# Attention and maxout on one core: group 3's q is loaded ahead of w1's second half, V follows its cast, and two pads and a relu change engines

## The chip, the cores and the metric

The kernel runs on one core of a Trainium2 chip. The metric is device time in microseconds of one execution. Engines are named as in the profile: PE is TensorE, DVE is VectorE, ACT is ScalarE, POOL is GpSimd, SP is SyncE. SP does no arithmetic here, it only issues transfers.

## The reference

Attention over 8 batches, 8 heads, 576 positions and head size 64, with a causal mask by blocks of 64, followed by a maxout layer over the 4608 tokens:

```python
scores = (1.0 / np.sqrt(D)) * np.matmul(q, k.transpose(0, 1, 3, 2))
scores = np.where(block_i >= block_j, scores, -1000000000.0)
attn = exp(scores - max) / (sum + 1e-09)
x = np.matmul(attn, v)              # then (B * S, H * D) = (4608, 512)
g = np.maximum(x @ w1, x @ w2)      # d_ff = 1024
out = g @ w_out                     # (4608, 512), float32
```

The kernel writes max(h1, h2) as relu(x (w1 - w2)) + x w2, so that the last step is `relu(x d) w_out + x m` with `d = w1 - w2` and `m = w2 w_out`, both made on the chip.

## The kernel before

**The work.** Heads are taken in pairs p = 0 to 31, four to a batch, and two pairs make a group g = 0 to 15. A group's q and k come from memory as float32 in one 576 KB transfer each (`load_qk`, L107), are cast to bf16 (`cast`, L147), transposed on PE (`transposes`, L358, 18 small matmuls for q and 18 for k) and copied out of PSUM (L372). Scores go through `tile_0`, `tile_1` and `tile_2` (L446 to L472) into PSUM and through exp on ACT (L407) into `aT`; POOL clears the masked corners (`mask`, L411). `av` (L482) multiplies by V and divides by the sum. `tile_2` reads `kz`, a copy of two key blocks with zeros between them, which `pad_keys` (L389) makes for each pair. V is loaded a batch at a time in five parts (`load_v`, L157), from POOL's queue.

**The maxout layer.** `load_w1` (L175) loads w1 in two halves of 1 MB from SP's queue. `diff_w(j)` (L184, j = 0 to 3) subtracts a quarter of w2 from a quarter of w1 on DVE. `h_unit(i, f)` (L226, f = 0 to 7) makes 128 of the 1024 columns of the relu for 512 tokens, in four matmuls (L233) and a relu out of PSUM (L238); f = 0 and 1 need `diff_w(0)`, 2 and 3 `diff_w(1)`, and so on. `m_unit` and `bT_unit` make `m`; `y_unit` makes 128 rows of the result. PSUM tiles of all these steps, the transposes' too, are taken in turn from one pool of four buffers (`ps_m`, tag "m"), so that a step waits until the tile four before it has been read out.

**The order.** Each engine runs its instructions in the order in which this program writes them (`manual_schedule`, L86). `fill(n)` (L334) takes the next units of the maxout layer from a list, whatever is ready, for about n matmuls of 512 columns; so attention's steps are written out by hand and the holes between them are filled. From L591 to L691 the first four groups are written out; from L693 a loop takes groups 3 to 15.

**What gates a transfer.** With `gated`, `load_qk` first writes one element of the new buffer with a memset, on POOL or on the engine given, and SP's transfer waits for it. A transfer is thereby placed behind what stands ahead of the memset on that engine:

```python
            if gated:
                (nc.gpsimd if gated is True else gated).memset(t[:, 0, :1], 0.0)
```

SP issues its transfers in program order, and a transfer that waits holds those behind it.

**Around the change.** Before, SP issues q and k of group 2, both halves of w1, then q and k of group 3, one behind the other. POOL casts q of group 2, issues two of V's parts for batch 1, pads pairs 4 and 5, issues the other three parts, clears the gates of group 4, and casts q and k of group 3. DVE runs `diff_w(0)`, `diff_w(1)`, a relu, `diff_w(2)`, a relu, `diff_w(3)`, two relus.

Of the kernel before, what the change touches and what calls it, by code (L numbers as in the profile page):

```python
# [10 lines left out]
AF = mybir.ActivationFunctionType  # L11
# [3 lines left out]
def kernel(  # L15
# [10 lines left out]
    nc = tc.nc  # L26
# [17 lines left out]
    RPP = S // NP  # L44
# [9 lines left out]
    NCH = 5  # L54
# [50 lines left out]
    dve, pool, act = nc.vector.tensor_copy, nc.gpsimd.tensor_copy, nc.scalar.copy  # L105

    def load_qk(g, queues, gated=False):  # L107
        b, u = divmod(g, GPB)
        for nm, src, queue in (("q", q, queues[0]), ("k", k, queues[1])):
            if queue is None or by_dma(nm, g):  # L110
                continue
            raws[nm, g] = t = raw.tile([P, 2, RPP * D], FP32, name=f"{nm}raw")
            if gated:
                (nc.gpsimd if gated is True else gated).memset(t[:, 0, :1], 0.0)
            queue.dma_start(
                out=t[:],
                in_=src[b, 4 * u:4 * u + 4].rearrange(
                    "(s h) (p t) d -> (h p) s (t d)", h=2, t=RPP),
            )
# [4 lines left out]
    def by_dma(nm, g):  # L124
        return g >= T_DMA.get(nm, NG)
# [21 lines left out]
    def cast(nm, g, parts):  # L147
        if by_dma(nm, g):
            return
        t = raws[nm, g].rearrange("p s (t d) -> p t s d", d=D)  # L150
        if (nm, g) not in qk_n:
            qk_n[nm, g] = qkn.tile([P, RPP, 2, D], BF16, name=f"{nm}n")
        n = qk_n[nm, g]
        for copy, j0, j1 in parts:
            copy(out=n[:, j0:j1], in_=t[:, j0:j1])  # L155

    def load_v(b, c):  # L157
        rows = min(P, S - c * P)
        nc.gpsimd.dma_start(  # L159
            out=vv_r[b % NV][P - rows:, c, :, :D],  # L160
            in_=v[b, :, c * P:c * P + rows, :].rearrange("h p d -> p h d"),
        )
# [12 lines left out]
    def load_w1(i):  # L175
        t = wraw.tile([P, NDM, 2 * WB], FP32, name="w1raw")
        nc.sync.dma_start(out=t[:], in_=w1r[:, :, 2 * i * WB:2 * (i + 1) * WB])
        for j in range(2):
            w1_raw[2 * i + j] = t[:, :, j * WB:(j + 1) * WB]
# [4 lines left out]
    def diff_w(j):  # L184
        nc.vector.tensor_sub(d_sb[:, :, j * WB:(j + 1) * WB], w1_raw[j], w2_sb[j])  # L185
# [8 lines left out]
    dve, pool, act = nc.vector.tensor_copy, nc.gpsimd.tensor_copy, nc.scalar.copy  # L194
    SP, ACT = nc.sync, nc.scalar
# [30 lines left out]
    def h_unit(i, f):  # L226
        if f == 0:
            g_tiles[i] = g_pool.tile([P, NFF, SPAN], BF16, name="g")
        g = g_tiles[i]
        t0 = i * SPAN  # L230
        pt = ps_m.tile([P, SPAN], FP32, name="ps_h", tag="m")
        for c in range(NDM):
            nc.tensor.matmul(  # L233
                pt[:], d_sb[:, c, f * P:(f + 1) * P], xT[:, c, t0:t0 + SPAN],
                start=(c == 0), stop=(c == NDM - 1),
            )
            if c == NDM - 1:
                nc.vector.tensor_scalar_max(g[:, f], pt[:], 0.0)  # L238
            yield

    def bT_unit(j):
# [92 lines left out]
    def fill(n):  # L334
        while n > 0:
            if not current:
                k = next((k for k, t in enumerate(todo) if t[2] <= done_tokens[0]), None)
                if k is None:
                    return max(0, n)
                current.append(todo.pop(k))  # L340
            t = current[0]
            next(t[1])
            n -= t[3]
            t[0] -= 1
            if not t[0]:
                current.pop()
        return 0
# [10 lines left out]
    def transposes(nm, g, copies):  # L358
        n = qk_n.pop((nm, g))
        pts = [ps_m.tile([P, RPP, NP], BF16, name=f"ps_{nm}T", tag="m") for _ in range(2)]  # L360
        for j in range(RPP):
            for i in range(2):
                r = slice(i * NP, (i + 1) * NP)
                nc.tensor.transpose(  # L364
                    pts[i][:, j, :], n[r, j].rearrange("p s d -> p (s d)"), ident[r, r],
                )

        def copy_out(which=(0, 1), part=(0, NP), copy=None):
            p0, p1 = part
            for i in which:  # L370
                t = (qT_r if nm == "q" else kT_r)[(2 * g + i) % NT]
                (copy or copies[i])(  # L372
                    out=t[:, p0 * RPP:p1 * RPP].rearrange("q (p j) -> q p j", j=RPP),
                    in_=pts[i][:, :, p0:p1].rearrange("q j p -> q p j"),
                )
        return copy_out

    def scores(p, ps, col, c, q0, w):
        qT, kT = qT_r[p % NT], kT_r[p % NT]
        k0 = min(c * P, S - P)  # L380
        for hh in range(2):
            r = slice(hh * D, (hh + 1) * D)
            nc.tensor.matmul(  # L383
                ps[:, hh, col:col + w], kT[r, k0:k0 + P], qT[r, q0:q0 + w],
                start=True, stop=True,
            )


    def pad_keys(p):  # L389
        nc.gpsimd.tensor_copy(  # L390
            out=kz_r[p % NT].rearrange("p (a c) -> p a c", c=BLK)[:, 0:3:2],
            in_=kT_r[p % NT][:, S - 3 * BLK:].rearrange("p (a c) -> p a c", c=BLK)[:, 0:3:2],
        )


    def corner_scores(p, ps, col):
        qT, kz = qT_r[p % NT], kz_r[p % NT]
        for k0, q0 in ((0, 384), (BLK, 512)):
            for hh in range(2):
                r = slice(hh * D, (hh + 1) * D)  # L400
                nc.tensor.matmul(  # L401
                    ps[:, hh, col:col + BLK], kz[r, k0:k0 + P], qT[r, q0:q0 + BLK],
                    start=(k0 == 0), stop=(k0 > 0),
                )

    def exp(p, ps, w, a0):
        nc.scalar.activation(  # L407
            out=aT_r[p % NA][:, :, a0:a0 + w], in_=ps[:, :, :w], func=AF.Exp, scale=scale,
        )

    def mask(p, a0, eng=None):  # L411
        (eng or nc.gpsimd).memset(aT_r[p % NA][BLK:, :, a0:a0 + BLK], 0.0)  # L412
# [33 lines left out]
    def tile_0(p):  # L446
        u = ps_s.tile([P, 2, 512], FP32, name="ps_s", tag="s")
        scores(p, u, 0, 0, 0, 512)
        return lambda masked: (exp(p, u, 512, 0), masked and mask(p, 0))
# [7 lines left out]
    def tile_2(p):  # L457
        u = ps_s.tile([P, 2, 512], FP32, name="ps_s", tag="s")
        corner_scores(p, u, 320)
        scores(p, u, 0, 2, 256, 320)  # L460
        scores(p, u, 384, 3, 448, P)

        def out(masked):
            exp(p, u, 512, 1024)
            nc.scalar.activation(
                out=aT_r[p % NA][BLK:, :, 1536:AW], in_=u[BLK:, :, 320:320 + BLK],
                func=AF.Exp, scale=scale,
            )
            if masked:
                mask(p, 1024)  # L470
                mask(p, 1344)
        return out  # L472

    def masks(p):
        for a0 in (0, 576, 1024, 1344):
            mask(p, a0)

    def region(*tiles, masked=True):
        for out in tiles:
            out(masked)  # L480
# [157 lines left out]
    load_qk(2, (SP, None), gated=nc.vector)  # L638
    load_qk(2, (None, SP))
    load_w1(0)  # L640
    load_w1(1)
    load_qk(3, (SP, SP))
    av(2, [2, 3, 4])
    burst_q3(3)
    mask(3, 1408)
# [1 line left out]
    x_out(0)  # L647
    av(3, [0, 1])
    cast("q", 2, ((pool, 0, RPP),))
    load_v(1, 0)  # L650
    load_v(1, 1)
    fill(8)
    av(3, [2, 3, 4])
    fill(8)
    x_out(1, 0, NCH, (act, dve))
    fill(4)
    transposes("q", 2, (dve, act))()
    cast("k", 2, ((act, 0, RPP),))
    fill(8)
    diff_w(0)  # L660
    diff_w(1)
    transposes("k", 2, (act, act))()
    pad_keys(4)
    pad_keys(5)
    for c in range(2, NCH):
        load_v(1, c)
    fill(4)
    load_qk(4, (SP, SP), gated=True)
    cast("q", 3, ((pool, 0, RPP),))
    cast("k", 3, ((pool, 0, RPP),))  # L670
    region(tile_0(4), tile_1(4), masked=False)
    fill(4)
    diff_w(2)
    fill(4)
    region(tile_2(4), tile_0(5), masked=False)
    diff_w(3)
    masks(4)
    fill(8)
    copy_out = transposes("q", 3, (dve, act))
    outs = tile_1(5), tile_2(5)  # L680
    copy_out()
# [1 line left out]
    fill(4)  # L683
    transposes("k", 3, (dve, act))()
    pad_keys(6)
    pad_keys(7)
    masks(5)
# [90 lines left out]
```

## Time and profile before

| | |
|---|---|
| median of 4 runs | 255.62 us (255.4 to 257.37) |
| profiled execution | 255.83 us |
| its span | 254.0 us |
| PE busy | 239.7 us, 94% |
| DVE, ACT, POOL busy | 150.8, 119.9, 119.2 us |
| granted PE clock | 1.0 |

The span runs from the first instruction to the last; the rest of the execution's time lies around it. Busy times are of each engine by itself, so they add up to far more than the span. DMA busy is the mean over 16 DMA engines. Times in the timelines count from the start of the span.

### The profile page before, as it was taken

The page shows a single profiled execution, that of the slowest core. Times are in us where ns is not written, and L with a number is a line of the kernel's source. Part 1 is how long each engine was busy: PE and PEld are TensorE (multiplying, and loading weights), DVE is VectorE, ACT ScalarE, POOL GpSimd, SP SyncE. Part 2 cuts the span into 40 slices and gives each one's busy share as a digit, 9 for nine tenths or more (in the row PEclk, how much of TensorE's full clock was granted, in tenths as well). Part 3 has the DMA queues.
Part 4 walks back from the last instruction along what each step waited for, and adds up shares of the span by engine and source line. Part 5 has one row for each costly group of instructions (what it writes and reads, how often), then busy time and mean ns, then how long its engine had stood idle before and what let it go on. Part 6 is the DMA issues. An engine that isn't in the chain of part 4 may idle for free.

```text
span 254.0 us, 6697 instructions
## 1 busy us (share of the span) xinstructions
PE 239.7 (94%) x2728; PEld 132.7 (52%) x2763; DVE 150.8 (59%) x303; ACT 119.9 (47%) x158; POOL 119.2 (47%) x280
## 2 busy tenths in 40 slices
PE   8787998998999999999999999999999999999995
PEld 3356853655455554545454545454545564444444
DVE  4977689666485367636753675357535754754521
ACT  2893297757675564646464646464645400000001
POOL 1970467579759556854685477547231100000000
PEclk9999999999999999999999999999999999999999
DMA  7999999699899999999999999999961311102123
GB/s 247 240 158 236 395 284 215 201 107 220 160 132 214 154 233 168 205 158 225 148 225 159 226 138 216 159 224 146 119 128 62 93 38 69 62 8 77 41 91 116
DMA packets 104863, 41.27 MB, mean 162 GB/s; under 512 B 89216, under 2 KB 93696, under 8 KB 104832
## 3 DMA queue, kind: packets, MB, share of 16 engines
q0 software_dynamic: 65376, 9.77, 57.7%
q1 hardware_dynamic: 39040, 30.42, 51.2%
q10 hardware_dynamic: 416, 0.66, 0.7%
q8 instruction: 21, 0.34, 0.6%
q14 instruction: 10, 0.08, 0.1%
HBM read 34.60 MB, written 9.44 MB: 173 GB/s over the span
## 4 chain that ended last, share of the span: by engine, by line
PE 85%; DMA 5%; DVE 4%; POOL 2%; issue 2%; ACT 1%; ACTq 0%
PE ps_y L275 35%; PE ps_h L233 24%; PE ps_o L498 11%; PE ps_s L383 8%; PE ps_M L256 3%; DMA vv<-in_v_dram 3%; DMA qraw<-in_q_dram 2%; PE ps_qT L364 2%; POOL vv L159 1%; DVE d_sb L185 1%; PE ps_y L290 1%; ACT aT L407 1%; PE ps_s L401 1%; PE ps_kT L364 1%; POOL xT L182 1%
## 5 line engine op out<-in xcount | busy, mean ns | idle before, releaser
L407 ACT ACTIVATE aT<-ps_s 128x1024 bf16<-128x1024 f32 (+2 forms) x100 | 95.6, 994 | 43.7 <-PE ps_s L383 30.6
L275 PE MATMUL ps_y<-wo_sb,g 128*128 128x512 bf16 x262 | 66.9, 379 | 2.6 <-issue 2.5
L233 PE MATMUL ps_h<-xT,d_sb 128*128 128x512 bf16 x277 | 66.9, 379 | 1.8 <-DVE g L238 0.8
L238 DVE TENSOR_SCALAR g<-ps_h 128x512 bf16<-128x512 f32 x72 | 49.5, 689 | 16.8 <-PE ps_h L233 16.8
L412 POOL MEMSET aT<- 64x128 bf16 x128 | 22.5, 199 | 63.5 <-ACT aT L407 62.8
L280 DVE COPY y<-ps_y 128x512 f32<-128x512 f32 x35 | 24.2, 691 | 45.9 <-PE ps_y L275 45.1
L498 PEld LDWEIGHTS <-aT 128*128 128x128 bf16 x960 | 37.4, 98 | 14.1 <-issue 0.4
L233 PEld LDWEIGHTS <-d_sb 128*128 128x128 bf16 x288 | 26.5, 98 | 32.1 <-issue 3.8
L275 PEld LDWEIGHTS <-g 128*128 128x128 bf16 x280 | 24.8, 98 | 30.2 <-issue 5.4
L498 PE MATMUL ps_o<-vv,aT 128*128 128x65 bf16 x960 | 39.7, 194 | 0.0
L275 PE MATMUL ps_y<-m_sb,xT 128*128 128x512 bf16 x135 | 37.3, 379 | 0.4 <-issue 0.2
L159 POOL DMA_DIRECT2D vv<-in_v_dram x40 | 33.9, 857 | 0.5
L383 PE MATMUL ps_s<-qT,kT 64*128 64x128 bf16 (+6 forms) x344 | 31.2, 280 | 2.9 <-ACT aT L407 1.1
L505 DVE TENSOR_TENSOR xp<-ps_o,rec 128x256 bf16<-128x256 f32 (+1 forms) x64 | 31.4, 491 | 2.2
L132 POOL DMA_DIRECT2D kb<-in_k_dram x40 | 29.4, 759 | 0.0
L504 DVE RECIPROCAL rec<-ps_o 128x4 f32<-128x4 f32 (+1 forms) x64 | 11.9, 187 | 25.4 <-PE ps_o L498 24.9
L295 ACT COPY y<-ps_y 128x256 f32<-128x256 f32 (+1 forms) x2 | 0.6, 319 | 49.3 <-PE ps_y L290 49.3
L155 POOL CAST qn<-qraw 128x1152 bf16<-128x1152 f32 (+1 forms) x15 | 16.5, 1102 | 11.2 <-DMA qraw<-in_q_dram 10.3
L372 ACT COPY qT<-ps_qT 128x576 bf16<-128x576 bf16 x15 | 9.6, 638 | 24.2 <-PE ps_qT L364 22.8
L275 PEld LDWEIGHTS <-xT 128*128 128x128 bf16 x140 | 12.7, 98 | 13.8 <-issue 0.8
L383 PEld LDWEIGHTS <-kT 64*128 64x128 bf16 x344 | 12.0, 94 | 13.3 <-issue 8.3
L372 DVE COPY qT<-ps_qT 128x576 bf16<-128x576 bf16 x17 | 12.7, 748 | 0.3 <-PE ps_qT L364 0.2
(57 smaller groups left out, 131.7 us busy)
## 6 DMA issues: line engine op xcount, KB each, us to landing
qraw<-in_q_dram SPq DMA_DIRECT2D x16, 576.0 KB, 5.0
out_dram<-y SPq DMA_DIRECT2D x35, 256.0 KB, 3.5
vv<-in_v_dram POOLq DMA_DIRECT2D x32, 128.0 KB, 6.1
kraw<-in_k_dram SPq DMA_DIRECT2D x5, 576.0 KB, 7.7
kb<-in_k_dram POOLq DMA_DIRECT2D x40, 72.0 KB, 6.4
w1raw<-in_moe_w_dram SPq DMA_DIRECT2D x2, 1024.0 KB, 10.7
xT<-in_moe_w_dram POOLq DMA_DIRECT2D x4, 256.0 KB, 6.5
wo_sb<-in_moe_w_out_dram POOLq DMA_DIRECT2D x2, 512.0 KB, 12.5
```

The source lines that it names most:

```text
L132: nc.gpsimd.dma_start(out=n[h * BLK:(h + 1) * BLK, :, s], in_=(q if nm == "q" else k)[b, 4 * u + 2 * s + h].rearrange("(j p) d -> p j d", ...
L159: nc.gpsimd.dma_start(out=vv_r[b % NV][P - rows:, c, :, :D], in_=v[b, :, c * P:c * P + rows, :].rearrange("h p d -> p h d"),)
L233: nc.tensor.matmul(pt[:], d_sb[:, c, f * P:(f + 1) * P], xT[:, c, t0:t0 + SPAN], start=(c == 0), stop=(c == NDM - 1),)
L238: nc.vector.tensor_scalar_max(g[:, f], pt[:], 0.0)
L275: nc.tensor.matmul(py[:], lhs, rhs, start=(n == 0), stop=(n == len(terms) - 1),)
L280: nc.vector.tensor_copy(out=y[:], in_=py[:])
L372: (copy or copies[i])(out=t[:, p0 * RPP:p1 * RPP].rearrange("q (p j) -> q p j", j=RPP), in_=pts[i][:, :, p0:p1].rearrange("q j p -> q p j"),)
L383: nc.tensor.matmul(ps[:, hh, col:col + w], kT[r, k0:k0 + P], qT[r, q0:q0 + w], start=True, stop=True,)
L407: nc.scalar.activation(out=aT_r[p % NA][:, :, a0:a0 + w], in_=ps[:, :, :w], func=AF.Exp, scale=scale,)
L412: (eng or nc.gpsimd).memset(aT_r[p % NA][BLK:, :, a0:a0 + BLK], 0.0)
L498: nc.tensor.matmul(po[:, gi, hh, :], a[:, hh, a0:a0 + P], vv[:, c, h0 + 2 * hh, :], start=(mm == 0), stop=(mm == n_mm - 1),)
L505: nc.vector.tensor_mul(xp[:, :, ts[0]:ts[0] + n, p % 2].rearrange("q s t d -> q t s d"), po[:, :, :, :D], rec[:, :n].to_broadcast([P, n, 2 ...
```

## The change

It touches the hand-written stretch before the loop only. SP's row of loads is written in two parts: q, k of group 2 and w1's first half as before; then, later in the program, q of group 3 with a gate on POOL behind group 2's cast, w1's second half, and k of group 3. The cast of group 3's q follows on POOL, and behind it all five parts of V for batch 1. Pads 4 and 5 go to DVE. The relu of `h_unit(0, 3)` goes to ACT. Two calls change place: the cast of group 2's k on ACT is written ahead of the transposes of its q, and `diff_w(3)` is written 4 units later. The matmuls and their order on PE are the same.

```diff
@@ h_unit
             if c == NDM - 1:
-                nc.vector.tensor_scalar_max(g[:, f], pt[:], 0.0)
+                if i == 0 and f == 3:
+                    nc.scalar.activation(out=g[:, f], in_=pt[:], func=AF.Relu)
+                else:
+                    nc.vector.tensor_scalar_max(g[:, f], pt[:], 0.0)
...
-    def pad_keys(p):
-        nc.gpsimd.tensor_copy(
+    def pad_keys(p, copy=pool):
+        copy(
...
     load_qk(2, (SP, None), gated=nc.vector)
     load_qk(2, (None, SP))
     load_w1(0)
-    load_w1(1)
-    load_qk(3, (SP, SP))
     av(2, [2, 3, 4])
...
     x_out(0)
     av(3, [0, 1])
     cast("q", 2, ((pool, 0, RPP),))
-    load_v(1, 0)
-    load_v(1, 1)
+    load_qk(3, (SP, None), gated=True)
+    load_w1(1)
+    load_qk(3, (None, SP))
+    cast("q", 3, ((pool, 0, RPP),))
+    for c in range(NCH):
+        load_v(1, c)
     fill(8)
     av(3, [2, 3, 4])
     fill(8)
     x_out(1, 0, NCH, (act, dve))
     fill(4)
+    cast("k", 2, ((act, 0, RPP),))
     transposes("q", 2, (dve, act))()
-    cast("k", 2, ((act, 0, RPP),))
     fill(8)
     diff_w(0)
     diff_w(1)
     transposes("k", 2, (act, act))()
-    pad_keys(4)
-    pad_keys(5)
-    for c in range(2, NCH):
-        load_v(1, c)
+    pad_keys(4, dve)
+    pad_keys(5, dve)
     fill(4)
     load_qk(4, (SP, SP), gated=True)
-    cast("q", 3, ((pool, 0, RPP),))
     cast("k", 3, ((pool, 0, RPP),))
     region(tile_0(4), tile_1(4), masked=False)
     fill(4)
     diff_w(2)
     fill(4)
     region(tile_2(4), tile_0(5), masked=False)
+    masks(4)
+    fill(4)
     diff_w(3)
-    masks(4)
-    fill(8)
+    fill(4)
     copy_out = transposes("q", 3, (dve, act))
```

## The prediction

> **What bounds the kernel now.** I read the page first, then the busy time by stretches, the waits, the chain in order of time, and the timelines of single queues. In all of them a group g is a pair of head pairs (2g, 2g+1); q3 and k3 are the q and k of group 3, h0 to h7 the eight `h_unit` calls of token span 0.
>
> ```profile
> span 254.0 us, 6697 instructions
> PE 239.7 (94%) x2728; PEld 132.7 (52%) x2763; DVE 150.8 (59%) x303; ACT 119.9 (47%) x158; POOL 119.2 (47%) x280
> DMA  7999999699899999999999999999961311102123
> ```
>
> TensorE is busy 94% of the span, and its matmuls are the same in both programs and in the same order. The change can only fill or widen TensorE's holes. The stretches say how large those are where the change lies (columns: length, then busy time of PE, PEld, DVE, ACT, POOL, then granted clock, DMA share, GB/s):
>
> ```profile
> 23.00:34.00 11.00, 9.63 (x150) 7.80 (x150) 7.19 (x17) 3.67 (x6) 3.06 (x4) 1.00 1.08 372
> 34.00:46.00 12.00, 10.83 (x110) 4.89 (x112) 10.59 (x13) 9.79 (x14) 8.97 (x22) 1.00 1.39 201
> 46.00:66.00 20.00, 18.33 (x319) 11.22 (x322) 11.75 (x28) 14.11 (x20) 14.91 (x36) 1.00 1.12 173
> ```
>
> TensorE idles 1.37, 1.17 and 1.67 us in them. The waits between 15 and 66 us name the causes:
>
> ```profile
> PEld L256 <- DMA wo_sb<-in_moe_w_out_dram: 1.5, 1, 1.5
> PE ps_h L233 <- DVE g L238: 0.8, 1, 0.8
> PE ps_qT L364 <- POOL qn L155: 0.2, 1, 0.2
> ```
>
> The first, up to 24.59 us, waits for w_out, which was queued before anything that moves here: untouched. The change can reach the other two, 0.78 us ahead of h4 and 0.17 us ahead of q3's transposes. The chain shows the larger one:
>
> ```profile
> 36.18 1.21 DVE d_sb L185
> 37.40 0.60 DVE g L238
> 38.00 2.02 DVE d_sb L185
> 40.01 0.61 DVE g L238
> 40.67 0.38 PE ps_h L233
> ```
>
> VectorE runs `diff_w(3)` ahead of h2's relu, and h4 takes the PSUM buffer that this relu frees. That `diff_w` took 2.10 us where its three siblings took 1.21 to 1.27. GpSimd's timeline says why:
>
> ```profile
> 29.68 1.76 POOL L159 DMA_DIRECT2D vv<-in_v_dram  x2
> 33.78 0.30 POOL L390 COPY kz<-kT 128x128 bf16<-128x128 bf16 x1 [2.35 <-ACT kT L372]
> 34.32 0.99 POOL L390 COPY kz<-kT 128x128 bf16<-128x128 bf16 x1 [0.24 <-ACT kT L372]
> 35.26 2.45 POOL L159 DMA_DIRECT2D vv<-in_v_dram  x3
> 37.74 1.19 POOL L155 CAST qn<-qraw 128x1152 bf16<-128x1152 f32 x1
> 39.12 1.90 POOL L155 CAST kn<-kraw 128x1152 bf16<-128x1152 f32 x1 [0.20 <-DMA kraw<-in_k_dram]
> ```
>
> **A lock.** q3's cast began at 37.74, `diff_w(3)` at 37.92; the diff lost 0.9 us, about what was left of the cast. k3's cast began inside the diff and ended at 41.02, which is 1.0 after the diff (40.02) where a free cast takes 1.14. The second pad, 0.99 us against 0.30, ended at 35.31 just after `diff_w(1)` (35.15). So whichever of the two engines starts second seems to stand until the first is through.
>
> **The change, part by part.** Times are those of the profiled execution: 255.83 us, of which 254.0 span and 1.83 around it; it lies 0.21 above the median of 255.62.
>
> *DMA order.* Before, SyncE issued q2, k2, both halves of w1, q3 and k3 from 21.87 to 26.7 us. By the issue view (issue plus time to landing) they landed in that order at 28.5, 30.0, 32.6, 35.5, 37.2 and 39.05: a queue emptied at 1.5 to 1.85 us per 576 KB and 2.6 to 2.9 per 1024 KB. Now q3 is gated by a GpSimd memset behind q2's cast, so q3, w1's second half and k3 are issued from about 29.9 (28.59 + 1.14 + the memset's 0.15). The queue still holds w1's first half until 32.6, so it does not run dry. By the same steps q3 lands at 34.1 to 34.5, w1's second half at 36.8 to 37.2, k3 at 38.3 to 39.05. Bounds for q3 by rows: a q load in quiet took 3.9 us (issued 44.67), which gives 33.8; q4's, beside V, took 7.6, which gives 37.5; q3's own 12.7, with 3 MB queued ahead, would give 42.6. I take 34.3, since what is ahead of it is counted. q2, k2 and w1's first half keep their place, at no cost.
>
> *GpSimd's row.* It was: q2's cast, two V issues, pads 4 and 5, three V issues, gates of q4 and k4, casts of q3 and k3. Now it is: q2's cast, gate of q3, q3's cast, five V issues, gates of group 4, k3's cast. q3's cast is ready at 34.4, but `diff_w(1)` runs until 35.15: by the lock it runs from 35.2 to 36.35 (free of the lock: 34.4 to 35.55; behind two pads as well: 35.5 to 36.65). Five V issues are 1.76 + 2.45 = 4.21, to 40.6. Gates 0.1. k3's cast 1.14, from 40.8 to 41.95, with `diff_w(3)` over by then (below). Before, it ended at 41.02. k3's transposes then start at 42.1, after 41.62 before: **+0.5**. With no lock at all they start at 41.2, −0.4; with the lock and the pads in front and the longest cast (1.90) at 43.0, +1.4.
>
> *VectorE's row.* Pads 4 and 5 come behind `diff_w(1)`. No such copy on VectorE is in the trace; it lies between the 0.09 of its memset (L205) and the 0.42 of a 128x256 cast (L261). I take 0.2 each by size: 35.15 to 35.55, ahead of the scores at 36.33 that read them, with 0.8 us of cover. If q3's cast wins the lock first, the pads wait until 36.4 and those scores lose 0.3. h0's relu (0.6) follows; `diff_w(2)` waits for w1's second half and runs 37.0 to 38.2 (before: 36.18 to 37.39, no wait); relus of h1 and h2 to 39.4. q3's transposes need h1's relu, done at 38.8: TensorE gets there at 38.81, so a tie. h4 needs h2's relu, done at 39.4, and starts at 39.88, where the scores ahead of it end: the 0.78 and the 0.17 are gone. `diff_w(3)` runs 39.4 to 40.65 beside V issues (`diff_w(2)` beside them took its plain 1.21), and h6, which needs it, is past 42.
>
> So the 0.95 us gained at q3's transposes and h4 is waiting time in front of k3's transposes. What counts is when those start; the 0.95 is spent there.
>
> *ScalarE.* h3's relu: no such row; 128x256 out of PSUM took 0.37 (L261), 128x640 0.69 (L541), so about 0.55, from 39.2 (end of an exp) to 39.8. k3's first transposes reuse its buffer, at 41.2 at the earliest: covered by 1.4 us. q3's copy, two exps and a corner behind it move from 42.25 to 42.7; the next exp was idle before for 1.4 us: nothing. k2's cast moves ahead of a qT copy, and starts at 30.15, when k2 has landed; the copy ends by 31.95, the next user of either is at 32.5: nothing, TensorE had followed the old cast (32.55) at 32.61.
>
> A rule that speaks against this part: the Trainium skill, "ScalarE: Activation LUTs", "Rules for kernel authors", gives relu to VectorE, as up to about three times faster in bf16. The trace's own relu reads f32 PSUM and takes 0.69 us, no faster than the ScalarE copies above. By the rule the relu would be an estimated 2.1 us and end at 41.3, still ahead of the 42.1 forecast for its reader, so the sum is the same by both. The same page ("Table sets: the hidden batching unit") has relu in one set with exp, so that no second table load is expected beside the one that the trace shows (1.28 us, at the start).
>
> *V and q4.* V's first two parts are now issued at 36.4 (before 29.68), the last at 39.9 (before 37.0). TensorE reads the first from 45.45, the last near 46.9. They took 9.6 (first, behind k3) and 7.2 to 7.6 us (the others): 46.0 at worst and 47.1 to 47.5. With TensorE itself 0.5 late, that is 0 to 0.1 us of wait; I take 0, since the 9.6 and 7.6 had k3, q3 and q4 beside them. q4 is issued at 40.8, not 37.84; it took 7.6 beside V, 3.9 in quiet: 44.7 to 48.4, and its transposes, at 47.1, need it by 45.8. The bytes on the engines up to there are the same, so I take its old 45.4, cost 0; the far end costs 2.
>
> **Sum.** 255.83 + 0.5 − 0.0 = 256.3 on the profiled execution, 256.1 on the median's scale; a tenth off for a lock that may hold only in part: 256.0. The delay then stays, since TensorE is at 147 of 150 us from 66 to 216.
>
> **The rivals.** *The gap is really filled* (0.24). No lock for q3's cast, k3's transposes at 41.2: 255.62 − 0.4 = 255.2; with a faster q3 (33.8) 254.8. For it: q3's old cast itself took 1.19 beside the diff. Against: 4.2 us of V issue stand between two casts that were adjacent. To beat 1% all 1.17 idle of this stretch and all 1.67 of the next would have to go: 252.8, 0.05 of this.
>
> *GpSimd's row is late, and the kernel slower* (0.19). Place: q3's cast, behind which V's issue, q4's gate and k3's cast stand. From a landing of 35.1 on, each us is one us for k3's transposes. At the 7.6 us of q4's row q3 lands at 37.5, its cast ends at 38.75, V is out at 43.0, k3's cast ends at 44.25, transposes 44.4: +2.8, 258.4. For it: q3, meant to come early, is now issued 5.4 us later than before (29.9 for 24.5); it is only its place in the queue that moves up. Against: the queue's steady steps.
>
> *w1's second half is late* (0.07): with 9.8 us (its sibling's) from 30.6 it lands at 40.4 and holds VectorE's relus, q3's transposes at 42.4 for 38.98: +3.4, 259.0. Nothing ahead of it is that large now.
>
> **How the numbers follow.** Forecast 0.50 (its own range 255.4 to 256.7), rivals 0.24, 0.19, 0.07. 1% is 2.56 us, about what a measurement of this kernel can tell from no change. Faster 0.05; slower 0.21, four fifths of the two late cases; within 0.74. The range 254.8 to 258.3 runs from the filled gap with a faster q3 to just short of the full late row, and holds the far ends of the longest cast and of q4.
>
> **What would show it.** Right: q3's cast ending near 36.3, V issue to 40.6, TensorE idle about 1 us before k3's transposes at 42.1, no wait at h4. Wrong: those transposes before 41.6, q3 landed after 35.1, or av(4) (L498, near 46) waiting for V.

## The result and the profile after

The changed kernel takes 256.51 us (median of 43 runs, 254.68 to 258.92) where the kernel before takes 255.35 (64 runs). The ratio is 1.0037, 95% interval 1.0023 to 1.0050: about 0.95 us slower, well within 1% (the plain medians differ by 1.16). Ratios leave out executions over 1.5% above the fastest of the same kernel, one here and three of the kernel with V ahead of q3's cast below. The profiled execution took 257.32 us, of which 255.5 are span; it lies 0.8 above its own median, so its rows are read for what waits for what, and the runs below for how much.

The head of the page, the busy time of each engine, and the DMA engines' busy share in 40 slices of the span:

```profile
span 255.5 us, 6701 instructions
PE 240.7 (94%) x2728; PEld 132.9 (52%) x2763; DVE 150.6 (59%) x304; ACT 120.3 (47%) x159; POOL 118.7 (46%) x279
DMA  7999999889999999999999999999952301202123
```

PE has the same work; what has changed is where it stands. The stretches (length, then busy PE, PEld, DVE, ACT, POOL, clock, DMA share, GB/s):

```profile
23.00:34.00 11.00, 10.69 (x175) 8.46 (x172) 7.49 (x17) 4.45 (x9) 1.39 (x3) 1.00 0.96 311
34.00:46.00 12.00, 9.69 (x94) 4.26 (x97) 10.11 (x14) 8.72 (x12) 9.88 (x21) 1.00 1.37 229
46.00:66.00 20.00, 18.18 (x321) 11.32 (x325) 12.41 (x28) 13.40 (x19) 14.58 (x30) 1.00 1.15 185
```

Between 34 and 46 us PE idles 2.31 us instead of 1.17, and the clock is at 1.00 throughout. The waits of PE from 30 to 50 us (total, times, longest) name the causes:

```profile
PE ps_kT L367 <- POOL kn L155: 1.0, 1, 1.0
PE ps_qT L367 <- POOL qn L155: 0.7, 1, 0.7
PE ps_h L233 <- DVE d_sb L185: 0.6, 1, 0.6
PE ps_qT L367 <- DVE g L241: 0.6, 1, 0.6
PE ps_s L404 <- DVE kz L393: 0.3, 1, 0.3
PE ps_y L278 <- issue: 0.2, 1, 0.2
```

The wait of h4 for VectorE's relu is gone. In its place stand k3's transposes (first row, for k3's cast on GpSimd), q4's transposes (second row), q3's transposes (fourth row, behind h1's relu) and the scores that read the pads (fifth row). The third row, h0's wait for `diff_w(0)`, is not new: the second profile of the kernel before, below, has it too. GpSimd's timeline (start, duration, in brackets the idle time before):

```profile
27.84 1.14 POOL L155 CAST qn<-qraw 128x1152 bf16<-128x1152 f32 x1 [4.48 <-DMA qraw<-in_q_dram]
28.92 0.10 POOL L114 MEMSET qraw<- 128x1 f32 x1
34.39 1.85 POOL L155 CAST qn<-qraw 128x1152 bf16<-128x1152 f32 x1 [5.37 <-DMA qraw<-in_q_dram]
36.19 4.19 POOL L159 DMA_DIRECT2D vv<-in_v_dram  x5
...
40.40 1.94 POOL L155 CAST kn<-kraw 128x1152 bf16<-128x1152 f32 x1
...
47.43 1.14 POOL L155 CAST qn<-qraw 128x1152 bf16<-128x1152 f32 x1 [2.25 <-DMA qraw<-in_q_dram]
```

After the gate at 28.92 GpSimd does nothing for 5.37 us, and then q3's cast, V's five issues and k3's cast stand back to back. The last row is q4's cast: GpSimd waits for q4, whose load could be issued only when V was out (40.51). VectorE's timeline beside it:

```profile
32.88 2.36 DVE L185 TENSOR_TENSOR d_sb<-w1raw,xT 128x1024 bf16<-128x1024 f32 x2 [1.39 <-DMA w1raw<-in_moe_w_dram]
35.16 1.23 DVE L393 COPY kz<-kT 128x128 bf16<-128x128 bf16 x2
36.31 0.68 DVE L241 TENSOR_SCALAR g<-ps_h 128x512 bf16<-128x512 f32 x1
37.62 1.23 DVE L185 TENSOR_TENSOR d_sb<-w1raw,xT 128x1024 bf16<-128x1024 f32 x1 [0.64 <-DMA w1raw<-in_moe_w_dram]
38.77 1.28 DVE L241 TENSOR_SCALAR g<-ps_h 128x512 bf16<-128x512 f32 x2
39.97 1.37 DVE L185 TENSOR_TENSOR d_sb<-w1raw,xT 128x1024 bf16<-128x1024 f32 x1
```

The two pads take 1.23 us, where two such copies alone take 0.29 (33.28 in the kernel with one operand, below): they stand until q3's cast is through (36.24). And `diff_w(2)` waits 0.64 us for w1's second half.

### The profile page after: what moved, and what is told of

Same layout as the page of the kernel before. It is cut to its first block, busy times and chain, and to the rows that moved or that the text cites. A ratio compares the mean times of both kernels' runs of the same rounds, so it can differ in the third digit from the quotient of the medians.

```text
span 255.5 us, 6701 instructions
## 1 busy us (share of the span) xinstructions
PE 240.7 (94%) x2728; PEld 132.9 (52%) x2763; DVE 150.6 (59%) x304; ACT 120.3 (47%) x159; POOL 118.7 (46%) x279
## 4 chain that ended last, share of the span: by engine, by line
PE 82%; DMA 7%; ACT 4%; POOL 3%; issue 2%; DVE 1%; POOLq 0%; ACTq 0%
PE ps_y L278 34%; PE ps_h L233 22%; PE ps_o L501 10%; PE ps_s L386 8%; DMA qraw<-in_q_dram 7%; ACT aT L410 3%; PE ps_w L356 3%; PE ps_qT L367 2%; POOL qn L155 2%; POOL vv L159 1%; PE ps_y L293 1%; PE ps_s L404 1%; PE ps_kT L367 0%; PE ps_xe L539 0%; DVE bT_sb L250 0%
## 5 line engine op out<-in xcount | busy, mean ns | idle before, releaser
L410 ACT ACTIVATE aT<-ps_s 128x1024 bf16<-128x1024 f32 (+2 forms) x100 | 95.6, 994 | 44.8 <-PE ps_s L386 33.1
L241 DVE TENSOR_SCALAR g<-ps_h 128x512 bf16<-128x512 f32 x71 | 48.8, 689 | 16.6 <-PE ps_h L233 16.6
L155 POOL CAST qn<-qraw 128x1152 bf16<-128x1152 f32 (+1 forms) x15 | 17.2, 1147 | 16.6 <-DMA qraw<-in_q_dram 16.6
## 6 DMA issues: line engine op xcount, KB each, us to landing
out_dram<-y SPq DMA_DIRECT2D x35, 256.0 KB, 3.5
xT<-in_moe_w_dram POOLq DMA_DIRECT2D x4, 256.0 KB, 6.3
```

The costliest lines, as they stand in the source:

```text
L410: nc.scalar.activation(out=aT_r[p % NA][:, :, a0:a0 + w], in_=ps[:, :, :w], func=AF.Exp, scale=scale,)
```

## The experiments

The theory was that GpSimd's row sets the time: V's 4.19 us of issue between q3's cast and what stands behind it, k3's cast and group 4's gate (the expectations call it the row theory). The rivals were the loads (the queue theory), issued at 29 us instead of 24 (w1's second half lands late), and the changes of engine (pads, relu).

**The kernel before, profiled again** (no edit).

> The kernel before, unchanged, profiled a second time, because the shown profile of it held a 1.5 us wait of TensorE for w_out near 24 us that the profile of the changed kernel did not hold. If that wait comes and goes from run to run (theory), M starts near 23.2 instead of 24.59 us, q3's transposes near 37.6, k3's near 40.2, av(4) near 44.1 and q4's transposes near 45.7, span near 253.2; the changed kernel's 39.50, 42.39, 46.22 and 48.63 are then late by 1.9 to 2.9 us, more than its median's 0.95. If the wait belongs to the kernel before and only the change removes it (rival), M starts at 24.6 again and the changed kernel's steps are late by 0.5 to 1.5.

Measured: 255.52 us (8 runs) beside 255.26; the profiled execution took 255.65, span 253.9. The first M matmuls start at 23.18 us, the wait for w_out is not there, and q3's, k3's and q4's transposes start at 38.35, 40.98 and 46.86. The wait comes and goes with the run and is not part of the change. Without it TensorE is early, and waits elsewhere. Its waits from 30 to 50 us:

```profile
PE ps_h L233 <- DVE g L238: 0.8, 1, 0.8
PE ps_h L233 <- DVE d_sb L185: 0.6, 1, 0.6
PE ps_qT L364 <- POOL qn L155: 0.3, 1, 0.3
```

That is 1.7 us of waits in 30 to 50 us, where the changed kernel has 3.4. The difference, 1.7, is the difference of the two profiled executions (257.32 and 255.65). The numbers forecast for q3's and k3's transposes (37.6, 40.2) were missed by 0.8, about the 0.6 that h0 now waits; q4's (45.7) was missed by 1.2. Beside this profile the changed kernel's three transposes are late by 1.15, 1.41 and 1.77 us, less than the 1.9 to 2.9 forecast. This profile is the base of the table below.

**SyncE's row alone** in two parts, with the gate, in the kernel before; everything else as before.

```diff
-    load_w1(1)
-    load_qk(3, (SP, SP))
     av(2, [2, 3, 4])
...
     cast("q", 2, ((pool, 0, RPP),))
+    load_qk(3, (SP, None), gated=True)
+    load_w1(1)
+    load_qk(3, (None, SP))
     load_v(1, 0)
     load_v(1, 1)
```

> The kernel before with only SyncE's row split: q3 gated behind q2's cast, then w1's second half, then k3; GpSimd's and VectorE's work otherwise in the old order and on the old engines. Queue theory: the whole delay of the changed kernel is here, 0.9 us over before or more (256.3 and up). Row theory: k3's cast and q4's gate stand where they stood, no wait at q4; w1's second half lands near 37.3, diff_w(2) and with it diff_w(3) and h2's relu move back by about a microsecond, so h4 waits longer: 0.2 to 0.9 us over before (255.5 to 256.2).

Measured: 258.86 us, ratio 1.014 (1.0101 to 1.0179), the costliest of all. w1's second half lands so late (39.3) that `diff_w(2)` starts at 39.45 after 2.91 us of idle time, and q3's transposes wait 2.12 us for the relu behind it. Part of the cost is not a wait. The clock in the stretch behind it:

```profile
39.00:41.00 2.00, 0.20 (x2) 0.10 (x2) 1.55 (x2) 0.49 (x1) 0.00 (x0) 1.00 2.12 193
41.50:44.50 3.00, 2.78 (x33) 1.20 (x27) 2.77 (x4) 2.50 (x4) 2.54 (x5) 0.50 1.29 279
```

PE stood from 39.2 to 41.33; from about 41.4 to 44.8 its granted clock was 0.50. Half speed for 3.4 us costs an estimated 1.7 us. Five of the six runs show a mean clock of 0.987 to 0.993; the sixth, at 1.0, took 257.03, still 1.7 above the kernel before.

**The engine parts alone**: pads on VectorE, the relu on ScalarE, k2's cast and `diff_w(3)` at their new places; SyncE's row and q3's cast as before. With the pads off GpSimd, V's five issues come together there, and group 4's gates behind them at 32 us.

```diff
     load_w1(0)
+    load_w1(1)
+    load_qk(3, (SP, SP))
     av(2, [2, 3, 4])
...
     cast("q", 2, ((pool, 0, RPP),))
-    load_qk(3, (SP, None), gated=True)
-    load_w1(1)
-    load_qk(3, (None, SP))
-    cast("q", 3, ((pool, 0, RPP),))
-    for c in range(NCH):
-        load_v(1, c)
+    load_v(1, 0)
+    load_v(1, 1)
...
     pad_keys(5, dve)
+    for c in range(2, NCH):
+        load_v(1, c)
     fill(4)
     load_qk(4, (SP, SP), gated=True)
+    cast("q", 3, ((pool, 0, RPP),))
     cast("k", 3, ((pool, 0, RPP),))
```

(The diff is against the changed kernel.)

> The kernel before with all of the change but SyncE's row and the place of q3's cast: pads 4 and 5 on VectorE, h3's relu on ScalarE, k2's cast ahead of the copy, diff_w(3) four units later. Row theory: these are harmless or of use: h4 waits no more (0.78 us), GpSimd without pads issues V's last three parts from 31.4 and opens q4's gate near 34; k3's cast, beside diff_w(3), ends near 41: 0.3 to 0.9 us below before (254.4 to 255.0). Engine theory (the delay comes from pads and relu on engines with two-input subtractions and exps around them): 0.3 to 1 us over before (255.6 to 256.3).

Measured: 255.75 us, ratio 1.0029 (1.0007 to 1.0051); its profiled execution, at 255.18, was faster than its median. h4's wait is gone, q3's and k3's transposes start at 37.87 and 39.95, but TensorE now waits 0.52 us for V: group 4's loads are issued right behind V's, and V comes late (the last kernel below moves them). The number lies in the range of the rival (255.6 to 256.3), and the forecast gain of 0.3 to 0.9 did not come. The last kernel below, with the same engine parts, is not slower than before: what costs here is an order of loads, not the engine parts.

**V ahead of q3's cast** in the changed kernel.

```diff
-    cast("q", 3, ((pool, 0, RPP),))
     for c in range(NCH):
         load_v(1, c)
+    cast("q", 3, ((pool, 0, RPP),))
```

> The changed kernel with V's five issues ahead of group 3's q cast on GpSimd instead of behind it; all else as changed. Row theory (the delay comes from V's 4.2 us of issue between q3's cast and what follows it, k3's cast and q4's gate): V's issue fits into GpSimd's idle time from 29 to 34 us, k3's cast ends near 40.5, q4 is issued near 36, the waits of 1.03 us at k3's transposes and 0.69 at q4's go, and the kernel is 0.9 to 1.7 us faster than the changed one (254.7 to 255.6). Queue theory (the delay comes from w1's second half and q3 being issued at 29 instead of 24): nothing gained, since w1's second half lands no earlier, and V's packets beside it may make it later: 256.3 to 257.5.

Measured: 256.51 us over all twelve runs, 256.23 without the three longest, ratio 1.0032 (1.0008 to 1.0057), as slow as the changed kernel. Both waits on GpSimd's casts are gone, as the theory has it, and the time is not: w1's second half lands at 38.2, and q3's transposes wait 1.28 us for h1's relu. The three longest runs, at 259.6 to 260.2, show a mean clock of 0.987 to 0.993; the profile, at 0.998, is not one of them. VectorE's row here:

```profile
35.75 0.68 DVE L241 TENSOR_SCALAR g<-ps_h 128x512 bf16<-128x512 f32 x1
38.26 1.22 DVE L185 TENSOR_TENSOR d_sb<-w1raw,xT 128x1024 bf16<-128x1024 f32 x1 [1.83 <-DMA w1raw<-in_moe_w_dram]
39.41 1.28 DVE L241 TENSOR_SCALAR g<-ps_h 128x512 bf16<-128x512 f32 x2
```

This suggests that one cause was covered by another; the two ungated kernels below test it.

**Group 4's loads ahead of V** in the changed kernel.

```diff
     cast("q", 3, ((pool, 0, RPP),))
+    load_qk(4, (SP, SP), gated=True)
     for c in range(NCH):
         load_v(1, c)
...
     fill(4)
-    load_qk(4, (SP, SP), gated=True)
     cast("k", 3, ((pool, 0, RPP),))
```

> The changed kernel with group 4's load written ahead of V's five issues on GpSimd, so that q4 and k4 are issued near 36.4 instead of 40.5. Row theory: the 0.69 us wait at q4's transposes goes and the 1.03 us at k3's stays: 0.5 to 0.8 us faster than the changed kernel (255.5 to 256.0), unless V, now behind q4 and k4 in the DMA engines, makes av(4) wait near 46. Queue theory: no change (256.3).

Measured: 256.56 us, ratio 1.0057 (1.0033 to 1.0081). q4's transposes no longer wait, but TensorE waits 1.1 us for V, and 1.7 us for h1's relu. What is issued behind the other is late; 0.7 us for q4 is exchanged for 1.1 us for V.

**The new order without the gate**: q3, w1's second half and k3 at the old place on SyncE, in the new order; GpSimd's row as in the changed kernel.

```diff
     load_w1(0)
+    load_qk(3, (SP, None))
+    load_w1(1)
+    load_qk(3, (None, SP))
     av(2, [2, 3, 4])
...
-    load_qk(3, (SP, None), gated=True)
-    load_w1(1)
-    load_qk(3, (None, SP))
     cast("q", 3, ((pool, 0, RPP),))
```

> The changed kernel, but q3, w1's second half and k3 are issued in their new order at the old place on SyncE (behind w1's first half, near 24 to 26 us) without the gate: only the order of the queue is new. Queue theory (the late issue at 29 us lets the queue run thin, so that w1's second half lands at 37.6 and DVE's second pair of differences starts late): w1's second half lands at 36.8 to 37.2, k3 by 38.5, time 255.6 to 256.0. Row theory (V's five issues between q3's cast and k3's cast set the time): landings alone move, k3's transposes still start about 42.3 and q4's about 48.5, time 256.3 to 256.7, as for the changed kernel.

Measured: 256.34 us, ratio 1.0038 (1.0022 to 1.0053), in the row theory's range. Its places are earlier than forecast: k3's and q4's transposes start at 41.37 and 47.26 (42.3 and 48.5), but TensorE's first M matmul too stands 0.73 earlier than in the profile of the changed kernel. The loads do come earlier: q3's cast starts at 33.64, and `diff_w(2)` waits for nothing. But the time that VectorE no longer waits is time in front of k3's transposes:

```profile
PE ps_kT L367 <- POOL kn L155: 1.4, 1, 1.4
PE ps_h L233 <- DVE d_sb L185: 0.3, 1, 0.3
PE ps_qT L367 <- POOL qn L155: 0.3, 1, 0.3
PE ps_s L404 <- DVE kz L393: 0.3, 1, 0.3
```

What the gate does to the queue is seen in the stretch of 30 to 32 us. First the changed kernel, then the ungated one, then V first with the gate:

```profile
30.00:32.00 2.00, 2.00 (x32) 1.63 (x30) 1.26 (x3) 1.10 (x3) 0.00 (x0) 1.00 0.99 322
```

```profile
30.00:32.00 2.00, 2.00 (x34) 1.60 (x33) 0.53 (x2) 1.10 (x3) 0.00 (x0) 1.00 1.04 391
```

```profile
30.00:32.00 2.00, 2.00 (x34) 1.61 (x32) 1.35 (x3) 1.74 (x3) 2.00 (x4) 1.00 0.69 154
```

The last number is GB/s: 391 with a full queue, 322 with loads issued at 29, and 154 in the third. In all profiles of this stretch, those without the gate move 382 to 394, those with the gate and V behind q3's cast 296 to 352, SyncE's row alone 192. The packets of the third (V first, gated) say that V is not what slows this stretch:

```profile
DMA  2211211111991939120930319269325779899989
DMA packets 140, 0.31 MB, mean 154 GB/s; under 512 B 3, under 2 KB 3, under 8 KB 140
q1 hardware_dynamic: 140, 0.31, 69.1%
```

The first row is the DMA engines' busy share in 40 slices of these 2 us. In the first half microsecond they stand nearly idle, and only from 31.5 us on are they busy throughout, though w1's first half lands only at 32.2. The packets are those of SyncE's queue (q1); V's, which are under 512 B, follow from 32 us on (1036 in the next 2 us). With V first and no gate the stretch moves 392. So the gate let the queue run nearly empty, and V's packets came behind that, beside the late loads.

**V first and no gate**: the last two edits together.

```diff
     load_w1(0)
+    load_qk(3, (SP, None))
+    load_w1(1)
+    load_qk(3, (None, SP))
     av(2, [2, 3, 4])
...
-    load_qk(3, (SP, None), gated=True)
-    load_w1(1)
-    load_qk(3, (None, SP))
-    cast("q", 3, ((pool, 0, RPP),))
     for c in range(NCH):
         load_v(1, c)
+    cast("q", 3, ((pool, 0, RPP),))
```

> V's five issues ahead of q3's cast, as in the first run of this list (256.51 us), but with q3, w1's second half and k3 issued at the old place on SyncE, ungated, in the new order. That is one difference from that first run, the gate. Gate theory (loads issued at 29 us, beside V's small packets, land late, where loads queued at 24 us are ahead of V): w1's second half lands by 36.9 instead of 38.2 less M's offset, VectorE waits for it no longer than 0.5, q3's transposes start near 37.9, k3's near 40.0, and the time is 254.9 to 255.4, 1.1 to 1.6 below the gated one. Rival, packets of V slow w1's second half wherever it stands in the queue: it lands at 37.5 or later, and the time stays within 0.5 of 256.5.

Measured: 255.39 us, ratio 1.0005 (0.9981 to 1.0028): level with the kernel before. w1's second half is there at 36.5 (`diff_w(2)` starts at 36.52 after 0.51 us of waiting; 38.26 with the gate), the wait for k3's cast is gone. What TensorE still waits for from 30 to 50 us:

```profile
PE ps_h L233 <- DVE qT L375: 0.8, 1, 0.8
PE ps_s L404 <- DVE kz L393: 0.4, 1, 0.4
PE ps_qT L367 <- DVE g L241: 0.3, 1, 0.3
```

The first row is a new price: VectorE's copy of q3 stands behind `diff_w(3)`, which took 1.84 us beside k3's cast. The four kernels make a square:

| ratio to before (median, us) | V behind q3's cast | V ahead of it |
|---|---|---|
| gated, issued at 29 us | 1.0037 (256.51) | 1.0032 (256.23) |
| not gated, issued at 24 us | 1.0038 (256.34) | 1.0005 (255.39) |

Either alone costs 0.8 to 1 us and both cost no more: V's issue holds k3's cast (and group 4's loads) and w1's second half holds the relus, side by side. Taking one away changes the ratio by 0.0005 at most; taking both, by 0.0032, or 0.8 us. The intervals (1.0023 to 1.0050, 1.0008 to 1.0057, 1.0022 to 1.0053, 0.9981 to 1.0028) overlap at their ends, so it is the times together with the waits of the profiles that show this, not the times alone.

**The relu back on VectorE**, otherwise the changed kernel.

```diff
-                if i == 0 and f == 3:
-                    nc.scalar.activation(out=g[:, f], in_=pt[:], func=AF.Relu)
-                else:
-                    nc.vector.tensor_scalar_max(g[:, f], pt[:], 0.0)
+                nc.vector.tensor_scalar_max(g[:, f], pt[:], 0.0)
```

> The changed kernel with h3's relu back on VectorE and everything else as it is. If the move of the relu is worth nothing because k3's cast releases k3's transposes later than any relu does (theory, as in the prediction), k3's transposes still start at the end of k3's cast and the time is within 0.3 of the changed kernel's 256.5. If the relu on VectorE, now behind a difference that itself waits for w1's second half, becomes the last release (rival), it ends after 42 us, k3's transposes start 0.3 to 0.7 later, and the time is 256.8 to 257.2.

Measured: 256.48 us, 0.03 from the changed kernel; its ratio to the runs of the kernel before beside it is 1.0058 (1.0032 to 1.0084), which overlaps the changed kernel's. The relu ends at 41.45, k3's transposes start at 41.90, still released by k3's cast (waiting 1.1 us for it). That part is worth nothing that these runs can resolve.

**One operand in place of two**: `diff_w` copies w1 and leaves out the subtraction of w2.

```diff
-        nc.vector.tensor_sub(d_sb[:, :, j * WB:(j + 1) * WB], w1_raw[j], w2_sb[j])
+        nc.vector.tensor_copy(out=d_sb[:, :, j * WB:(j + 1) * WB], in_=w1_raw[j])
```

> The changed kernel with the difference of w1 and w2 replaced by a copy of w1 alone (it leaves out the subtraction): VectorE then reads one operand from SBUF instead of two. Lock by the two-operand difference (theory): q3's and k3's casts on GpSimd take 1.14 to 1.2 us instead of 1.85 and 1.94, the pads 0.2 to 0.3 instead of 1.23. A lock by any VectorE work on SBUF, or by DMA traffic at those moments (rival): the casts stay at 1.8 or above. The time is no more than 0.5 below the changed kernel's in either case, as V's issue stays where it is.

Measured: 255.58 us, ratio 1.0006 (0.9987 to 1.0025), 0.9 below the changed kernel; forecast was 0.5 at most. GpSimd's and VectorE's rows:

```profile
33.67 1.14 POOL L155 CAST qn<-qraw 128x1152 bf16<-128x1152 f32 x1 [5.82 <-DMA qraw<-in_q_dram]
34.76 4.31 POOL L159 DMA_DIRECT2D vv<-in_v_dram  x5
39.03 0.58 POOL L114 MEMSET qraw<- 128x1 f32 x1
39.07 0.55 POOL L114 MEMSET kraw<- 128x1 f32 x1
39.11 1.48 POOL L155 CAST kn<-kraw 128x1152 bf16<-128x1152 f32 x1
```

```profile
33.28 0.29 DVE L393 COPY kz<-kT 128x128 bf16<-128x128 bf16 x2
...
36.22 0.81 DVE L185 CAST d_sb<-w1raw 128x1024 bf16<-128x1024 f32 x1 [1.51 <-DMA w1raw<-in_moe_w_dram]
...
38.14 1.44 DVE L185 CAST d_sb<-w1raw 128x1024 bf16<-128x1024 f32 x1
```

q3's cast took 1.14 here, but VectorE was through before it began, so it says nothing of two operands against one. k3's cast does: it and the gates ahead of it (0.58 for 0.10) ran into the last copy, which itself took 1.44 where its sibling took 0.81. The theory that it takes two operands is wrong: a copy of one locks too. What does not lock is a relu that reads PSUM: in the kernel with V first and no gate, two of them (1.28 us, as ever) ran into k3's cast of 1.14 us. The run also prices the lock at q3's cast: V's issue starts at 34.76 instead of 35.43 in the ungated kernel, whose first M matmul stands within 0.06 us of this one's, and k3's transposes at 40.64 instead of 41.37. That part of the price, 0.7 us, is mixed with the shorter copies, so why the gain was larger than forecast is not settled.

**The engine parts with group 4's loads behind q3's cast**, run twice.

```diff
-    load_qk(4, (SP, SP), gated=True)
     cast("q", 3, ((pool, 0, RPP),))
+    load_qk(4, (SP, SP), gated=True)
```

(against the kernel with the engine parts alone)

> The kernel with the engine parts only (pads on VectorE, one relu on ScalarE, SyncE's row as before), with group 4's loads issued behind q3's cast instead of ahead of it, as a candidate for a version faster than both. If the 0.52 us that TensorE waited for V there came from q4's and k4's packets running ahead of V's (theory), that wait goes and the time is 255.0 to 255.3, level with the kernel before or 0.2 faster. If V's own issue time sets it (rival), the wait stays and group 4, issued 4 to 5 us later, makes q4's transposes wait: 256 to 256.5.

> The kernel with the engine parts and group 4's loads behind q3's cast once more, since its interval against the kernel before touched 1. If it is really faster, its median is again 0.2 to 0.6 below the kernel before; if the first result was luck, it is within 0.15 of it.

Measured: 254.84 us, ratio 0.9985 (0.9970 to 1.0000), and 254.70, ratio 0.9983 (0.9962 to 1.0004): 0.4 to 0.5 below the kernel before both times, each with an interval that ends at 1 or just above, so the gain is likely and not proven. It is the fastest kernel of this study; the one with group 4's early gate was 0.7 above the kernel before. V's wait is gone, as the theory said, and q4's transposes wait 0.6 to 0.8, as the rival said; the sum is a gain. The rows of the second run:

```profile
PE ps_qT L367 <- POOL qn L155: 0.8, 1, 0.8
PE ps_kT L367 <- POOL kn L155: 0.2, 1, 0.2
```

**All profiles together.** PE's waits from 30 to 50 us, added up as the waits view prints them, against those of the kernel before profiled again (1.7 us; 255.65 us):

| kernel | waits, us | more than before | profiled execution, more than before |
|---|---|---|---|
| changed kernel | 3.4 | +1.7 | +1.67 |
| V first, gated (with 1.5 for w_out) | 3.5 | +1.8 | +1.47 |
| group 4 ahead of V | 3.7 | +2.0 | +2.03 |
| ungated order | 2.3 | +0.6 | +0.29 |
| V first, ungated | 1.5 | −0.2 | −0.26 |
| relu on VectorE | 2.1 | +0.4 | +0.71 |
| engine parts | 1.2 | −0.5 | −0.47 |
| the same, group 4 later, first and second run | 1.0, 1.0 | −0.7, −0.7 | −0.58, −0.89 |

In these nine profiles the waits of 20 us account for the time to 0.35 us. Three profiles are not in the table and fit less well. SyncE's row alone has 1.4 us more of waits and 3.54 more time; the clock's 1.7 covers most of the rest. The kernel with the copy has 0.7 more and 0.27 more time. The first profile of the kernel before has, with its 1.5 for w_out, 1.2 more and only 0.18 more time; where it won back the rest is open. Single executions of one kernel spread by 1.5 to 5 us, so the medians, not this table, say how much a kernel is worth.

## Why the prediction was right, and where it was off

It said 256.0 us and a change of +0.4; measured were 256.51 and about +0.95. The likeliest case was the one that came in its main line: the hole ahead of h4 is filled, V's issue stands between q3's and k3's casts, and TensorE waits 1.03 us in front of k3's transposes, where about 1 was forecast. The delay itself is more than twice the forecast, because waits that stood in the sum at nothing came on top: 0.69 for q4, 0.55 at q3's transposes, 0.29 for the pads. That k3's transposes start so near the forecast place (42.39 for 42.1) is in part luck: TensorE reached the first M matmul at 23.91 in this profile, 0.7 earlier than in the base, so that against the second profile of the kernel before they are 1.4 us late and not 0.5. None of the three signs of being wrong came: q3 landed before 35.1, those transposes started after 41.6, and av(4) did not wait for V. Point by point:

- *DMA order.* q3 landed at 34.2 (forecast 34.3). w1's second half landed at 37.56, forecast 36.8 to 37.2, 3.3 us behind q3 where the step was 2.6 to 2.9. The step that failed is "the queue still holds w1's first half until 32.6, so it does not run dry": that half landed at 32.8, and yet from 30 to 32 us the queue moved 322 GB/s where the full one moves 391, and with V first and the gate only 154. Ungated, `diff_w(2)` did not wait at all. Here too the places are nearer than the step deserves: the load was issued at 29.46, where the rival counted on 30.6, and took 8.1 us (7.9 to 8.6 in the three other profiles with the gate and V behind q3's cast).
- *GpSimd's row.* q3's cast ended at 36.24 (36.35), V was out at 40.4 (40.6), and then k3's cast took 1.94 us, not the 1.14 forecast "with `diff_w(3)` over by then". It was not over, since it came behind the late `diff_w(2)` (39.97 to 41.34 for 39.4 to 40.65). k3's transposes started at 42.39, not 42.1. Here the two late rows meet through the lock.
- *q4.* The term "the bytes on the engines up to there are the same, so I take its old 45.4, cost 0" was mis-sized: issued at 40.51, q4 took 6.8 us to land (47.3), and its transposes waited 0.69. The 2 us kept for the range covered it. From 41.0 to 41.6 us all 645 packets that moved were V's, from 41.6 to 43 all but 16 of 1055; q4 moved only when V was nearly through.
- *Pads.* The pads lost the lock to q3's cast, and the scores that read them lost 0.29: the case that was bounded at 0.3 but not taken.
- *q3's transposes* were called a tie and waited 0.55, with h1's relu behind the late `diff_w(2)`. *h4* did not wait, as forecast.
- *ScalarE.* h3's relu took 0.59 us (0.55 forecast) and is free, shown by the run with it back on VectorE. The rule weighed there (the Trainium skill, "ScalarE: Activation LUTs", "Rules for kernel authors") gives relu to VectorE with a figure for bf16. For this relu out of f32 PSUM the trace does not bear it out: it took 0.68 us on VectorE.
- *The base.* The shown profile of before had 1.5 us of waiting for w_out, which the second profile does not have. It has no part in the change, as the prediction said, but it hid 0.6 us of waiting at h0, and the prediction's places were counted from it.

Of the rivals, the filled gap did not come, since V's issue stands where it was seen to stand. "GpSimd's row is late" had the right place and the wrong cause: q3 landed on time. "w1's second half is late" came by 0.4 to 0.8 us in the changed kernel and nearly in full with SyncE's row alone: 258.86 us where 259.0 was worked out, though 1.7 of it is a clock that no step had foreseen.

What stays open: why V's packets went ahead of q4's, and how the two queues share the engines. One kernel of the square (V first, gated) was profiled in an execution with the w_out wait, so its landing times are compared in absolute time only.

## What to carry to other kernels

A gate that holds back a transfer can let the queue run empty, even while the last transfer ahead of it has not landed: count not only what is ahead of it when it is issued, but whether the queue still runs at its full rate until its data flow. Where two late rows run side by side, undoing one of them shows nothing; undo both before a cause is called innocent. And before a profile is taken as the base, take a second one: a wait that comes and goes at one place hides others further on.

## What the hardware showed

- A GpSimd cast and a VectorE copy or difference that both work in SBUF run one after the other, to about 0.2 us: casts of 1.85 and 1.94 us for 1.14 in the changed kernel, two pads in 1.23 for 0.29, a gate's memset in 0.58 for 0.10, a one-operand copy in 1.44 for 0.81. V's five issues took 4.19 to 4.31 us with such work beside them. The Trainium skill, "GPSIMD Engine Reference", "Key points", tells of contention for shared interfaces with VectorE instructions that have two SBUF inputs or run in a 2-port performance mode. The rows agree for the difference, which has two such inputs; in which mode the copy ran, no row shows. They also show that the loser stands until the winner is through.
- In the profile of SyncE's row alone an idle time of PE of 2.1 us (39.2 to 41.33) was followed by a granted clock of 0.50 for 3.4 us; the mean clock was 0.987 to 0.993 in five of its six runs. With V first and the gate three of twelve runs show the same, but none of them is the profiled one, so what preceded it there is not seen. Single runs of the kernel before (257.09 and 257.34 us) and of the changed one (257.55 and 258.43) show 0.993 too. The Trainium skill, "TensorE: Matmul & The Clock Gate", "Why this matters for your kernels", warns of gaps above about 3 us; here the clock fell behind a shorter one. If the gap is the cause, which no run tests by itself, a wait of 2 us costs an estimated 4.
